# Retention followed by a gated feed-forward block: moving the second tile's attention ticks, two small vector operations and a stream of stores

## The chip, the cores and the metric

The kernel runs on one core of a Trainium2 chip. The metric is the device time of one execution in microseconds. The times shown are medians of several executions.

## The reference

Two blocks follow each other. The first is retention: for each of 8 batches and 8 heads, with 576 positions and a head width of 64, the scores of queries and keys are scaled, multiplied by a decay that falls with the distance and is zero for later positions, and multiplied with the values. The second is a gated feed-forward block on the 4608 x 512 result.

```python
scores = scale * np.matmul(q, k.transpose(0, 1, 3, 2))
ret = scores * Dmat[None, :, :, :]        # gamma_h ** (i - j) for i >= j, else 0
attn_out = np.matmul(ret, v)
x = attn_out.transpose(0, 2, 1, 3).reshape(B * S, H * D)      # 4608 x 512
g, val = x @ w_gate, x @ w_val            # 512 -> 1536 each
out = (g * sigmoid(g) * val) @ w_out      # 1536 -> 512
```

All of it is in float32.

## The kernel before

Every engine works through its instructions in the order in which the Python code writes them (`manual_schedule`), so the place at which a function is called sets what stands behind what on each engine.

**Tiles.** Tokens are worked on in five tiles. The first (n = 0) is computed plainly. The other four (n = 1 to 4, 1024 tokens each) use a fast scheme of matrix multiplication that needs fewer products: each of the three thirds of the hidden columns (`qd` 0 to 2; called thirds 0, 1 and 2 in the text) takes 26 products with the up weights, and the down weights take 26 more. The tables UP and DOWN list, one line a product ("step"), which sums of inputs and weights it needs and what becomes of its result. `up_step` and `down_step` do one step each. One of the four PSUM banks takes the product; VectorE, ScalarE and GpSimd add it into partial results.

**The second tile is special.** At n = 1 the sums of the up weights are formed for the first time, by GpSimd (`w_sums`, L785 and L953) and ScalarE (`negated`, L943, which writes the negated operand into the very slot in which GpSimd then makes the sum). They lie in 13 slots, and slots 8 and higher are used again several times in a third. As each step's operand is used, it is also stored to DRAM (`up_ops`, L986), from where the later tiles fetch it. So a slot may be overwritten only when its store has landed. In the UP table the operand of step 13, for instance, is slot 9; line 15 has `nad 9 1 3`, which overwrites slot 9 for step 18; line 16 makes slot 11 for step 19.

The down operands are fetched from DRAM in all tiles (L880, by SyncE, called SP in the profile) into a ring of eight places. In the second tile the first eight fetches are called at the up steps 21, 22 and 25 of third 2.

**Ticks.** Attention for later tiles goes on between the steps. One tick (`tick`) is for one pair of heads of one batch, t: TensorE does the values of pair t-2, the new states of t-1 and the scores of t-1 (L531 to L572); then a list of `pieces` for VectorE and ScalarE is run one by one behind the following steps: `copies`, `outputs` (`to_x`), `own` (mask the scores), `pairs`, `odd`, `evens` with `keys`, then the transposes of the new pair's q and k on VectorE (L489, into qT and kT), and, together with the transpose of k, `next_load(t)`, which calls `load(t + 2)` on SP: eight transfers of q and k (L293), one of k by rows and one of v (L298). The q and k transfers overwrite the buffer that the transposes of pair t have just read. The next tick's scores need qT and kT.

In an up phase a step runs one piece (`part_on`), except next to lines with five or more results (after steps 17 and 18 none); a down step runs three (`go_on(3)`).

**Where the ticks stand.** `merge` spreads ticks evenly among steps. In the second tile third 0 has no ticks; `load` is called there after steps 6 and 14 only. Ticks 12 to 17 fall among the 52 up steps of thirds 1 and 2: before index 0, 9, 17, 26, 35 and 43 of these. Ticks 18 to 21 fall before down steps 2, 7, 13 and 19:

```python
merge((0.0, ticks(done, cut)), (0.5, ups))
if n == 1:
    for i, f in reversed(list(zip((2, 7, 13, 19), ticks(cut, upto), strict=True))):
        downs.insert(i, f)
```

`down_step` begins with the sums of its own line (`hops`, on VectorE, every third step on GpSimd), then the matmuls, then the reads of the bank, then the pieces. `up_step` issues the store right behind the step's matmuls, from ScalarE's queue.

Of the kernel before, what the change touches and what calls it, by code (L numbers as in the profile page):

```python
# [17 lines left out]
ALU = mybir.AluOpType  # L18
# [136 lines left out]
def kernel(  # L155
# [32 lines left out]
    nc = tc.nc  # L188
# [40 lines left out]
    xr, sr = outer[:, 0, 256 : 256 + L], outer[:, 0, 256 + L : 256 + 2 * L]  # L229
# [110 lines left out]
    last_near = const.tile([P, HP, L], F32, name="last_near")  # L340
# [105 lines left out]
    ret_last = const.tile([P, L], F32, name="ret_last")  # L446
# [128 lines left out]
    def masked(i):  # L575
        p, sr, (ret, ret_last, state) = i % HP, last_scores(i), places(i)

        def own():
            nc.vector.tensor_tensor(out=ret, in0=sc, in1=near[:, 2 * p : 2 * p + 2].unsqueeze(2).to_broadcast([P, 2, NFULL, L]),
                                    op=ALU.mult)  # L580

        def copies():
            (nc.vector.tensor_copy if vector(i + 1) else nc.scalar.copy)(out=even, in_=z[:, 0])

        odd_states = state[:, 1:].rearrange("p (c r) d -> p c r d", r=2)[:, :, 1]

        def pairs():

            nc.vector.tensor_tensor(out=ret_last, in0=sr, in1=last_near[:, p], op=ALU.mult)
            at = odd_states  # L590
            nc.vector.scalar_tensor_tensor(out=at, in0=even, scalar=step[:, p : p + 1], in1=z[:, 1], op0=ALU.mult, op1=ALU.add)

        def odd():
            at = odd_states
            for c in range(1, NFULL):
                nc.vector.scalar_tensor_tensor(out=at[:, c], in0=at[:, c - 1], scalar=step[:, HP + p : HP + p + 1],
                                               in1=at[:, c], op0=ALU.mult, op1=ALU.add)

        def evens():
            at = state[:, 0 : NC - 1].rearrange("p (c r) d -> p c r d", r=2)  # L600
            nc.vector.scalar_tensor_tensor(out=at[:, :, 1], in0=at[:, :, 0], scalar=step[:, p : p + 1], in1=even,
                                           op0=ALU.mult, op1=ALU.add)

        return [copies, own, [pairs, odd, evens]]

    def to_x(i):
        b, p = divmod(i, HP)
# [65 lines left out]
    def tick(t, lo=HP, hi=NP, spread=False, then=None):  # L673
        go_on(len(pieces))
        if hi == HP:

            if lo <= t - 1 < hi:
                scores(t - 1, True)
                new_states(t - 1)
                pieces.extend(masked(t - 1))  # L680
                go_on(3)
            if lo <= t - 2 < hi:
                own_values(t - 2)
            for f in transposes(t) if lo <= t < hi else ():
                f()
            if t + 1 == HP:
                split(0)
            if lo <= t - 2 < hi:
                earlier_values(t - 2)
                if t == HP:  # L690
                    rounding(2)
                    rounding(3)
                to_x(t - 2)[0]()
            if t + 1 == HP:
                rounding(0)
            return
        if lo <= t - 2 < hi:
            own_values(t - 2)
        if lo <= t - 1 < hi:
            new_states(t - 1)  # L700
        if lo <= t - 2 < hi:
            earlier_values(t - 2)
        if lo <= t - 1 < hi:
            scores(t - 1, t - 2 < lo)
        if lo <= t - 1 < hi and whole(t - 2) and not whole(t - 1):
            decay(slice(0, H), slice(0, H), half[1])
        copies, *masks = masked(t - 1) if lo <= t - 1 < hi else (lambda: None,)
        keys, *new = transposes(t) if lo <= t < hi else (lambda: None,)
        outputs = to_x(t - 2)[0] if lo <= t - 2 < hi else lambda: None
        late = needed(1) - 4 <= t < needed(1) - 2 or light(t - 2)  # L710
        if late and masks:
            own, (pairs, odd, evens) = masks
            pieces.extend([lambda: (copies(), outputs(), own()), [pairs, odd, lambda: (evens(), keys())]])
        elif late:
            pieces.append(lambda: (copies(), outputs(), keys()))
        else:
            pieces.extend([lambda: (copies(), keys()), outputs])
            pieces.extend(masks)
        if then and new:
            pieces.extend(new[:-1])  # L720
            pieces.append(lambda: (new[-1](), then()))
        else:
            pieces.extend(new)
            pieces.extend([then] if then else [])
        if not spread:
            go_on(len(pieces))
# [239 lines left out]
    def up_step(n, qd, i):  # L966
        label, opens, xslot, _, wslot, _, ops = up[i]
        busy = n == 1
        if qd == 0:
            done = lambda i: X_FIRST + (min(3 * i, 2 * i + 2, i + 6) if busy else i)  # L970
            x_sums(n, done(i), done(i + 1), busy)
        if busy:
            if i > 1:
                w_sums(qd, i)
            w = up_view(qd)(wslot)
        else:
            w = operand()[:, 0:512].rearrange("p (g x) -> p g x", g=2)
        rhs = x_view(n)(xslot)
        b = bank(label, i == 0)
        for gv in range(2):  # L980
            for c in range(2):
                m = nc.tensor.matmul(b[:, gv * TB : (gv + 1) * TB], w[:, gv, ts(c, P)], rhs[:, c, :],  # L982
                                     start=(opens and gv == 0 and c == 0), stop=(c == 1), skip_group_check=True)
        stepped.append(m)
        if busy:
            nc.scalar.dma_start(out=up_ops[qd][i].rearrange("p (g x) -> p g x", g=2), in_=w)  # L986
            if i in (20, 23) and qd + 1 < NQ:
                first_sums(qd + 1, *((0, 2) if i == 20 else (2, 4)))
            if i == 24 and qd + 1 < NQ:
                negated(qd + 1, 1)  # L990
                w_sums(qd + 1, 1)
            if 0 < i < N - 1:
                negated(qd, i + 1)
            if qd + 1 == NQ:
                for _ in range({21: 3, 22: 2, N - 1: 3}.get(i, 0)):
                    fetch()
        else:
            fetch()

        def result(o, src, negative, vector):  # L1000
            s = io[:, (silus[0] % 4) * TB : (silus[0] % 4 + 1) * TB]
            silus[0] += 1
            nc.scalar.activation(out=s, in_=src[:, 0:TB], func=AF.Silu, scale=-1.0 if negative else 1.0)  # L1003
            dst = hid[:, qd, o // 4, o % 4]
            if negative:
                return lambda: nc.vector.scalar_tensor_tensor(out=dst, in0=src[:, TB : 2 * TB], scalar=-1.0, in1=s,  # L1006
                                                              op0=ALU.mult, op1=ALU.mult)
            if vector:
                return lambda: nc.vector.tensor_tensor(out=dst, in0=src[:, TB : 2 * TB], in1=s, op=ALU.mult)
            nc.gpsimd.tensor_tensor(out=dst, in0=src[:, TB : 2 * TB], in1=s, op=ALU.mult)  # L1010

        reads(ops, b, busy, result, i > N // 2)
        if qd + 1 == NQ and i + 1 == N:
            while products:
                products.pop(0)[1]()
        if max(len(line[-1]) for line in up[i : i + 2]) < 5:
            part_on()

    def down_step(n, i):
        label, opens, slot, hops, ops = down[i]  # L1020
        for op in hops:
            add(nc.gpsimd if i % 3 == 1 and op[0] != "nad" else nc.vector, op, hid_view)
        w = operand().rearrange("p (q x) -> p q x", q=NQ)
        lhs = hid_view(slot)
        b = bank(label, i == 0)
# [14 lines left out]
        if n + 1 == NTILE and i + 1 == N:  # L1040
# [6 lines left out]
                queue.dma_start(out=out[rows + m * P : rows + (m + 1) * P, d * TB : (d + 1) * TB], in_=at[:, ts(m, TB)])  # L1047
            return
        reads(ops, b, False, result)
        at = 2 * (i - (N - 1 - X_FIRST // 2))  # L1050
        if 0 <= at < X_FIRST and n + 1 < NTILE:
            x_sums(n + 1, at, at + 2, True)
# [3 lines left out]
    def merge(*lists):  # L1056
        merged = [((i + d) / len(l), j, f) for j, (d, l) in enumerate(lists) for i, f in enumerate(l)]
        for _, _, f in sorted(merged, key=lambda e: e[:2]):
            f()
# [79 lines left out]
    for n in range(1, NTILE):  # L1139
# [10 lines left out]
                                      mybir.DependencyInfo(mybir.DependencyClass.Sync, mybir.DependencyReason.DATA), reason="loads in turn")  # L1150
                    load(FIRST + i // 14)
        downs = [lambda i=i: down_step(n, i) for i in range(N)]
        merge((0.0, ticks(done, cut)), (0.5, ups))
        if n == 1:

            for i, f in reversed(list(zip((2, 7, 13, 19), ticks(cut, upto), strict=True))):
                downs.insert(i, f)
            merge((0.5, downs))
        else:
            merge((0.0, ticks(cut, upto)), (0.5, downs))  # L1160
        done = upto

# [29 lines left out]
```

## Time and profile before

| | |
|---|---|
| median of the runs | 1050.15 us (1048.26 to 1051.46, 3 runs) |
| profiled execution | 1046.57 us, its span 1044.8 us |
| granted TensorE clock | 0.998 |
| second tile, third 0 of up | 175.6 to 222 us |
| second tile, third 1 | 222 to 274.4 us |
| second tile, third 2 | 274.4 to 324.3 us |
| second tile, down | 324.3 to about 406 us |
| stores of the up operands | 78, 256 KB each, 3.0 us from issue to landing |
| fetches of the down operands | 104, 384 KB each, 3.4 us to landing |

Times of the profile are in microseconds from the start of its span. In the timelines, a row has its start, its length, the engine (PE is TensorE's matmuls, PEld its weight loads, DVE VectorE, ACT ScalarE, POOL GpSimd, SP SyncE; a q behind the name means its sequencer, which issues transfers), the line of the code, what is written from what is read, how often, and in brackets the idle time before it with what ended it. In the lists of waits, an engine, the line and what it waited for are followed by the total, the number of times and the longest. A matmul of one step shows as 8 or 12 records. The idle time of an engine that is not the bound costs nothing.

### The profile page before, as it was taken

To read this page: it belongs to the slowest core of one execution; us is meant where nothing else is said; L and a number is where in the kernel's file an instruction comes from. 1 tells how busy PE (TensorE), PEld (TensorE's weight loads), DVE (VectorE), ACT (ScalarE), POOL (GpSimd) and SP (SyncE) were. 2 spreads that over 40 slices of the span, in tenths; PEclk is the share of its full clock that TensorE was granted. 3 is DMA by queue.
4 is the path that set the end of the run, shared out by engine and by line. 5 is a ranking of instruction groups with operands and counts; after the bars stand their busy time and mean duration, and the time that the engine had idled before them with its cause. 6 is when DMAs were issued, how large, how long until landed. Compare 5 with 4: busy or idle time off the path is not lost.

```text
span 1044.8 us, 21507 instructions
## 1 busy us (share of the span) xinstructions
PE 1025.3 (98%) x8448; PEld 842.7 (81%) x8448; DVE 648.1 (62%) x1063; ACT 295.2 (28%) x646; POOL 401.8 (38%) x347
## 2 busy tenths in 40 slices
PE   6999999999999999999999999999999999999998
PEld 5444555888887888888888888888888888888887
DVE  5578878677767857655468786425476644344644
ACT  4365423243633322132322102222120022231110
POOL 2002367767566035712223048312250483222505
PEclk9999999999999999999999999999999999999999
DMA  9999868776779788765676776545554565555553
GB/s 249 243 280 265 195 196 278 196 209 181 199 195 249 204 216 245 196 166 156 184 219 150 221 184 222 153 137 155 152 173 144 150 201 151 152 153 160 181 161 100
DMA packets 310380, 199.10 MB, mean 191 GB/s; under 512 B 220168, under 2 KB 254984, under 8 KB 310280
## 3 DMA queue, kind: packets, MB, share of 16 engines
q1 hardware_dynamic: 279000, 161.51, 57.2%
q10 hardware_dynamic: 31280, 36.22, 10.4%
q8 instruction: 67, 1.10, 0.4%
q14 instruction: 33, 0.27, 0.1%
HBM read 157.56 MB, written 40.11 MB: 189 GB/s over the span
## 4 chain that ended last, share of the span: by engine, by line
PE 79%; DVE 2%; issue 1%; ACT 0%; DMA 0%; ACTq 0%; DVEq 0%
PE bankC L982 13%; PE bankE L982 12%; PE bankA L982 12%; PE bankB L982 12%; PE bankA L1028 6%; PE bankB L1028 6%; PE bankC L1028 6%; PE bankE L1028 6%; PE outer L531 1%; PE inner L572 1%; PE outer L558 1%; PE inner L542 1%; DVE rest L919 1%; DVE rest L785 0%; PE outer L566 0%
## 5 line engine op out<-in xcount | busy, mean ns | idle before, releaser
L919 POOL TENSOR_TENSOR rest<-rest 128x512 f32<-128x512 f32 x65 | 91.7, 1416 | 298.4 <-DVE rest L919 276.8
L1003 ACT ACTIVATE io<-rest 128x256 f32<-128x256 f32 x180 | 74.9, 417 | 321.9 <-DVE rest L919 277.2
L982 PE MATMUL bankC<-rest,arena 128*128 128x256 f32 x544 | 129.0, 380 | 0.0
L982 PE MATMUL bankA<-rest,arena 128*128 128x256 f32 x544 | 128.7, 379 | 0.0
L785 POOL TENSOR_TENSOR arena<-arena 128x512 f32<-128x512 f32 (+1 forms) x72 | 111.8, 1565 | 39.9 <-DMA up<-arena 26.5
L982 PE MATMUL bankE<-rest,arena 128*128 128x256 f32 x512 | 121.4, 380 | 1.0 <-DVE rest L919 1.0
L982 PE MATMUL bankB<-rest,arena 128*128 128x256 f32 x512 | 121.2, 379 | 0.0
L1010 POOL TENSOR_TENSOR arena<-rest,io 128x256 f32<-128x256 f32 x72 | 52.1, 729 | 166.7 <-ACT io L1003 166.7
L982 PEld LDWEIGHTS bankA<-rest,arena 128*128 128x128 f32 x544 | 103.2, 190 | 14.5 <-issue 0.5
L982 PEld LDWEIGHTS bankC<-rest,arena 128*128 128x128 f32 x544 | 102.9, 190 | 14.5 <-POOL arena L785 0.3
L982 PEld LDWEIGHTS bankE<-rest,arena 128*128 128x128 f32 x512 | 97.0, 190 | 14.6 <-DVE rest L919 1.4
L982 PEld LDWEIGHTS bankB<-rest,arena 128*128 128x128 f32 x512 | 97.0, 190 | 13.3
L785 POOL TENSOR_TENSOR rest<-rest 128x256 f32<-128x256 f32 (+1 forms) x66 | 67.8, 1048 | 102.0 <-DVE rest L419 62.0
L919 DVE TENSOR_TENSOR rest<-bankB,rest 128x512 f32<-128x512 f32 x72 | 48.9, 687 | 67.4 <-PE bankB L982 49.3
L919 DVE TENSOR_TENSOR rest<-bankC,rest 128x512 f32<-128x512 f32 x72 | 48.8, 685 | 66.5 <-PE bankC L982 45.6
L919 DVE TENSOR_TENSOR rest<-bankA,rest 128x512 f32<-128x512 f32 x72 | 48.8, 686 | 62.9 <-PE bankA L982 45.5
L919 DVE TENSOR_TENSOR rest<-bankE,rest 128x512 f32<-128x512 f32 x71 | 48.1, 686 | 61.8 <-PE bankE L982 46.6
L1006 DVE SCALAR_TENSOR_TENSOR arena<-rest,io 128x256 f32<-128x256 f32 x84 | 57.2, 682 | 11.3 <-ACT io L1003 11.3
L1028 PE MATMUL bankA<-arena 128*128 128x256 f32 x252 | 58.0, 380 | 1.3 <-DVE arena L785 1.3
L1028 PE MATMUL bankB<-arena 128*128 128x256 f32 x252 | 58.5, 381 | 0.0
L1028 PE MATMUL bankC<-arena 128*128 128x256 f32 x252 | 58.1, 380 | 0.0
L1028 PE MATMUL bankE<-arena 128*128 128x256 f32 x252 | 57.9, 379 | 0.0
(189 smaller groups left out, 1624.6 us busy)
## 6 DMA issues: line engine op xcount, KB each, us to landing
arena<-up SPq DMA_DIRECT2D x234, 256.0 KB, 2.7
arena<-dn SPq DMA_DIRECT2D x104, 384.0 KB, 3.4
up<-arena ACTq DMA_DIRECT2D x78, 256.0 KB, 3.0
dn<-rest SPq DMA_DIRECT2D x78, 128.0 KB, 1.8
out_dram<-rest SPq DMA_DIRECT2D x31, 256.0 KB, 5.6
qk<-in_q_dram SPq DMA_DIRECT2D x108, 72.0 KB, 2.8
qk<-in_k_dram SPq DMA_DIRECT2D x108, 72.0 KB, 2.3
rest<-in_moe_w_out_dram ACTq DMA_DIRECT2D x6, 1024.0 KB, 6.4
```

The source lines that it names most:

```text
L531: m = nc.tensor.matmul(value(i, hl, c), s["v"][rows, at], ret[rows, c % 2 if whole(i) else hl, c // 2], start=start, stop=start, skip_grou ...
L542: nc.tensor.matmul(z[half[hl], r, c], s["kn"][chunk(i, hl, 2 * c + r, i < HP)], s["v"][rows, at], start=True, stop=True, skip_group_check= ...
L558: nc.tensor.matmul(xr[half[hl]] if c + 1 == NC else value(i, hl, c), state[half[hl], c, :], s["qT"][half[hl], column(i, hl, c)], start=Fal ...
L572: nc.tensor.matmul(sc[chunk(i, hl, 2 * c + r)[0], r if whole(i) else hl, c], kT[half[hl], at], qT[half[hl], at], start=True, stop=True, sk ...
L785: eng.tensor_tensor(out=dst, in0=srcs[0], in1=srcs[1], op=ALU.add if op[0] == "add" else ALU.subtract)
L919: eng.tensor_tensor(out=at(op[1]), in0=at(op[2]), in1=at(op[3]), op=ALU.add if op[0] == "add" else ALU.subtract)
L982: m = nc.tensor.matmul(b[:, gv * TB : (gv + 1) * TB], w[:, gv, ts(c, P)], rhs[:, c, :], start=(opens and gv == 0 and c == 0), stop=(c == 1 ...
L1003: nc.scalar.activation(out=s, in_=src[:, 0:TB], func=AF.Silu, scale=-1.0 if negative else 1.0)
L1006: return lambda: nc.vector.scalar_tensor_tensor(out=dst, in0=src[:, TB : 2 * TB], scalar=-1.0, in1=s, op0=ALU.mult, op1=ALU.mult)
L1010: nc.gpsimd.tensor_tensor(out=dst, in0=src[:, TB : 2 * TB], in1=s, op=ALU.mult)
L1028: nc.tensor.matmul(b[:, m * TB : (m + 1) * TB], lhs[:, qd, ts(m, P)], w[:, qd], start=(opens and qd == 0 and m == 0), stop=(qd == NQ - 1), ...
```

## The change

Four things are done.

- The last scores' mask (`ret_last`) becomes a piece of its own, `last`. In the ticks of the second tile it runs with `own`, which now also stands ahead of `outputs`; in later ticks it stays with `pairs`.
- The stores of the up operands are issued by SP instead of ScalarE.
- The sums of down step i + 1 are written behind the reads of step i, ahead of its pieces, in all four tiles (`hid_sums`).
- The second tile's ticks 12 to 17 stand before index 0, 7, 15, 25, 33 and 39 of the 52 up steps, tick 18 before down step 1 instead of 2.

```diff
@@ -584,9 +584,11 @@
 
         odd_states = state[:, 1:].rearrange("p (c r) d -> p c r d", r=2)[:, :, 1]
 
+        def last():
+            nc.vector.tensor_tensor(out=ret_last, in0=sr, in1=last_near[:, p], op=ALU.mult)
+
         def pairs():
 
-            nc.vector.tensor_tensor(out=ret_last, in0=sr, in1=last_near[:, p], op=ALU.mult)
             at = odd_states
             nc.vector.scalar_tensor_tensor(out=at, in0=even, scalar=step[:, p : p + 1], in1=z[:, 1], op0=ALU.mult, op1=ALU.add)
 
@@ -601,7 +603,7 @@
             nc.vector.scalar_tensor_tensor(out=at[:, :, 1], in0=at[:, :, 0], scalar=step[:, p : p + 1], in1=even,
                                            op0=ALU.mult, op1=ALU.add)
 
-        return [copies, own, [pairs, odd, evens]]
+        return [copies, own, [last, pairs, odd, evens]]
 
     def to_x(i):
         b, p = divmod(i, HP)
@@ -709,13 +711,14 @@
         outputs = to_x(t - 2)[0] if lo <= t - 2 < hi else lambda: None
         late = needed(1) - 4 <= t < needed(1) - 2 or light(t - 2)
         if late and masks:
-            own, (pairs, odd, evens) = masks
-            pieces.extend([lambda: (copies(), outputs(), own()), [pairs, odd, lambda: (evens(), keys())]])
+            own, (last, pairs, odd, evens) = masks
+            pieces.extend([lambda: (copies(), own(), last(), outputs()), [pairs, odd, lambda: (evens(), keys())]])
         elif late:
             pieces.append(lambda: (copies(), outputs(), keys()))
         else:
             pieces.extend([lambda: (copies(), keys()), outputs])
-            pieces.extend(masks)
+            for own, (last, pairs, *rest_of) in [masks] if masks else []:
+                pieces.extend([own, [lambda: (last(), pairs()), *rest_of]])
         if then and new:
             pieces.extend(new[:-1])
             pieces.append(lambda: (new[-1](), then()))
@@ -983,7 +986,7 @@
                                      start=(opens and gv == 0 and c == 0), stop=(c == 1), skip_group_check=True)
         stepped.append(m)
         if busy:
-            nc.scalar.dma_start(out=up_ops[qd][i].rearrange("p (g x) -> p g x", g=2), in_=w)
+            nc.sync.dma_start(out=up_ops[qd][i].rearrange("p (g x) -> p g x", g=2), in_=w)
             if i in (20, 23) and qd + 1 < NQ:
                 first_sums(qd + 1, *((0, 2) if i == 20 else (2, 4)))
             if i == 24 and qd + 1 < NQ:
@@ -1016,10 +1019,14 @@
         if max(len(line[-1]) for line in up[i : i + 2]) < 5:
             part_on()
 
+    def hid_sums(i):
+        for op in down[i][3]:
+            add(nc.gpsimd if i % 3 == 1 and op[0] != "nad" else nc.vector, op, hid_view)
+
     def down_step(n, i):
         label, opens, slot, hops, ops = down[i]
-        for op in hops:
-            add(nc.gpsimd if i % 3 == 1 and op[0] != "nad" else nc.vector, op, hid_view)
+        if i == 0:
+            hid_sums(0)
         w = operand().rearrange("p (q x) -> p q x", q=NQ)
         lhs = hid_view(slot)
         b = bank(label, i == 0)
@@ -1047,6 +1054,8 @@
                 queue.dma_start(out=out[rows + m * P : rows + (m + 1) * P, d * TB : (d + 1) * TB], in_=at[:, ts(m, TB)])
             return
         reads(ops, b, False, result)
+        if i + 1 < N:
+            hid_sums(i + 1)
         at = 2 * (i - (N - 1 - X_FIRST // 2))
         if 0 <= at < X_FIRST and n + 1 < NTILE:
             x_sums(n + 1, at, at + 2, True)
@@ -1150,13 +1159,16 @@
                                       mybir.DependencyInfo(mybir.DependencyClass.Sync, mybir.DependencyReason.DATA), reason="loads in turn")
                     load(FIRST + i // 14)
         downs = [lambda i=i: down_step(n, i) for i in range(N)]
-        merge((0.0, ticks(done, cut)), (0.5, ups))
         if n == 1:
 
-            for i, f in reversed(list(zip((2, 7, 13, 19), ticks(cut, upto), strict=True))):
+            for i, f in reversed(list(zip((0, 7, 15, 25, 33, 39), ticks(done, cut), strict=True))):
+                ups.insert(i, f)
+            merge((0.5, ups))
+            for i, f in reversed(list(zip((1, 7, 13, 19), ticks(cut, upto), strict=True))):
                 downs.insert(i, f)
             merge((0.5, downs))
         else:
+            merge((0.0, ticks(done, cut)), (0.5, ups))
             merge((0.0, ticks(cut, upto)), (0.5, downs))
         done = upto
```

In the order of the built program, SP then has a `load` after steps 2, 12 and 22 of third 1 (before: 2, 14, 24) and after steps 4, 12 and 20 of third 2 (before: 5, 14, 24), and the store of the step that follows stands behind each.

## The prediction

> **What bounds the kernel now.** I read the page's busy times and chain first, then the waits of TensorE alone, then the timelines of the second tile (175.6 to about 406 us of the span), where all but one part of the change lies. From the page:
>
> ```profile
> PE 1025.3 (98%) x8448; PEld 842.7 (81%) x8448; DVE 648.1 (62%) x1063; ACT 295.2 (28%) x646; POOL 401.8 (38%) x347
> PE 79%; DVE 2%; issue 1%; ACT 0%; DMA 0%; ACTq 0%; DVEq 0%
> ```
>
> TensorE is the bound. The change leaves its 4240 matmuls as they are, so it can only remove or add holes. The second tile's holes, in the table of TensorE's waits (us in total, times, longest):
>
> ```profile
> PE inner L572 <- issue: 2.3, 1, 2.3
> PE bankA L1028 <- DVE arena L785: 1.3, 1, 1.3
> PE outer L566 <- DVE kT L489: 1.1, 1, 1.1
> PE bankE L982 <- DVE rest L919: 1.0, 1, 1.0
> ```
>
> They lie at 331.9, 360.7, 272.6 and 191.3 us; from 406 us on TensorE is full except at the very end. Together they are 5.8 us: all that can be won, 0.55%.
>
> What can be lost shows in SP. Its waits have the line below, and its timeline one whole `load` (start, us):
>
> ```profile
> SPq L293 <- DVE kT L489: 95.5, 19, 13.6
> ...
> 313.98 8.77 SPq L880 DMA_DIRECT2D arena<-dn  x5
> 327.78 2.21 SPq L293 DMA_DIRECT2D qk<-in_q_dram  x4
> 330.04 2.18 SPq L293 DMA_DIRECT2D qk<-in_k_dram  x4
> 332.26 1.47 SPq L298 DMA_DIRECT2D kn<-in_k_dram  x1
> 333.78 0.62 SPq L298 DMA_DIRECT2D v<-in_v_dram  x1
> ```
>
> A `load` first holds SP until VectorE has transposed kT (the buffer it overwrites), then for 6.6 us of issuing (5.3 to 5.8 where kn takes 0.4 to 0.5 us as in the other ticks; I use 5.8). Now the way of one store, step 13 of third 1, through the timelines of ACT, POOL and PE (step 19 is the last line):
>
> ```profile
> 248.43 0.33 ACTq L986 DMA_DIRECT2D up<-arena  x1
> 250.54 0.63 ACT L943 ACTIVATE arena<-arena 128x512 f32<-128x512 f32 x1
> 251.25 1.27 POOL L953 TENSOR_TENSOR arena<-arena 128x512 f32<-128x512 f32 x1 [3.61 <-ACT arena L943]
> 253.21 2.74 POOL L919 TENSOR_TENSOR rest<-rest 128x512 f32<-128x512 f32 x2 [0.68 <-DVE rest L919]
> 255.90 1.27 POOL L785 TENSOR_TENSOR arena<-arena 128x512 f32<-128x512 f32 x1
> 258.64 1.89 PE L982 MATMUL bankE<-rest,arena 128*128 128x256 f32 x8
> ```
>
> The store reads slot 9 of the weights' sums. Slot 9 is then overwritten for step 18 (ACT negates, POOL subtracts), and POOL makes step 19's operand only after that and two more sums: at 257.2, with TensorE there at 258.6. The spare time is 1.4 us. That these engines do wait for landings, the same waits between 175 and 325 us say:
>
> ```profile
> POOL arena L785 <- DMA up<-arena: 26.5, 9, 5.1
> ACT arena L943 <- DMA up<-arena: 14.4, 7, 4.2
> ```
>
> **What the Trainium skill says.** DMA: Bandwidth & Descriptors, "Anatomy of one DMA": a DMA's semaphore waits are held on the sequencer that issues it, the DMA engines never wait. The trace agrees: the 95.5 us above are SP's own. The same page, "Issuing engines are not separate DMA queues": SP and ACT feed the same 16 engines, and two issuers save only issuing time. The trace has both queues (161.51 and 36.22 MB) but no run here shows them merged. Runtime: NRT & Kernel Launch, "Instruction fetch mechanics": instructions come in 16 KiB blocks of 256, the next fetched while the current runs. The instruction queue's 67 packets of 1.10 MB agree, and I take the hole of 2.31 us inside a tick's matmuls, which nothing released, for a block that came late.
>
> **The change part by part.** Steps of a third start 1.73 us apart (256.91, 258.64, 260.36); a full tick takes 2.56 us, tick 13, which has no values to do, 1.4.
>
> Down sums a step ahead: the same additions stand ahead of the next pieces of a tick instead of behind them. The hole of 1.35 us at 360.7 goes; cover for the pieces that are now later is a down step of 2.6 us: gain 1.4 with crumbs.
>
> Last scores masked earlier: one VectorE row of 0.23 us a tick, behind `own` instead of ahead of `pairs`. TensorE waits for neither: nothing, both ways within 0.2.
>
> Ticks at other steps: pieces run one per step (none after steps 17 and 18 of a third), `load` with the last. Ticks 13 to 17 move 2, 2, 1, 2 and 4 steps ahead. Tick 15 gets two steps instead of one between kT and its scores: the 1.1 us goes. Tick 17 now follows tick 16's kT with none between: a new wait of 0 to 2.5 us (from 1.1 with one step, plus 1.73, less what VectorE is quicker there); it falls into item 4 below and isn't counted twice. The late block of instructions may or may not come again, as the boundaries fall elsewhere: half, 1.2. The bank wait at 191.3 follows ACT, which loses its stores: half, 0.5. Gains in all: 4.2 (2.5 to 5.8).
>
> Stores on SP: ACT loses 78 issues of mostly 0.33 to 0.6 us; ACT is busy 16 to 23 us of each third of about 50, so that alone gives no more than the 0.5. On SP each store stands in program order behind any `load` issued at an earlier step. A `load` follows steps 2, 12 and 22 of third 1 and 4, 12 and 20 of third 2. The time from the step's end to kT was, before, 1.2, 3.4, 4.8, 3.8, 1.9 and 5.3 us (SP's start of L293 less the end of TensorE's step); for the new places I take 1.2, 2.5, 4, 2.5, 2 and 3. A store lands 3.0 us after issue (page, median), dn 3.4. From the end of the step:
>
> 1. Third 1, after step 2: store 3 leaves at 1.2 + 5.8 + 0.3 = 7.3, lands 10.3; negation and sum (0.63 + 1.27 + 0.1) to 12.3. It is step 8's operand, due at 5 steps + tick 13 = 10.0. Cost 2.3.
> 2. After step 12: store 13 leaves at 8.6, lands 11.6, sum of step 18 at 13.6, then 2.74 + 1.27 on POOL: 17.6. Step 19 is due at 6 steps + tick 14 = 12.9. Cost 4.7.
> 3. Third 2, after step 4: store 6 leaves at 9.1, lands 12.1, sum at 14.1; step 10 is due at 5 steps + tick 16 = 11.2. Cost 2.9.
> 4. After step 12: as 2 with kT at 2.0: 17.1 against 12.9. Cost 4.2.
> 5. After step 20: here the first down operands (L880) also stand behind the `load`; before, they went ahead of it, at 313.98. The first leaves at 3 + 5.8 + 0.5 = 9.3, lands 12.7; down step 0 is due 5 steps on, at 8.6. Cost 4.1.
> 6. The two `load`s of third 0 (after steps 6 and 14) and the one after step 22: spare time about equals the delay; 1 in all.
>
> Sum 19.2. Less 4.2: +15.0. The profiled execution took 1046.6 (span 1044.8 and 1.8 around it): 1061.6. The median of the runs lies 3.6 above that execution, so 1065.
>
> Bounds: stores landing in 2.0 us and kT half a us sooner take about 1.6 from each of items 1 to 5 (11 left, less 5.8: +5); landing in 5 us, which the timeline's v transfers of 4.4 us (page) ahead of them in the same queue allow, adds 2 to each (29, less 2.5: +27).
>
> **The rivals.** *The spare time holds (faster).* POOL and ACT are idle for half of the tile, and third 1's other sums have 3 to 4 us in hand. If kT came at once and the queue cleared within 4 us of a step's end, every item but 2 would vanish and the holes alone would decide: 1046. Deciding point: a store no more than 2 us later than ACT issued it. Against it: 5.8 us of issuing alone is over that.
>
> *Only the ticks count.* Stores turn out free, tick 17's wait and item 5's late operand give back the gains: about 1050, the same. Against it is the same figure.
>
> *The wait spreads (much slower).* ACT's negation waits for the landing in program order, and the SiLUs behind it, VectorE's products and the reading of banks wait with it; kT is then later and the next `load` too. Each item grows by 3 us or more: 1080 to 1090. For it: ACT waited 277 us for VectorE over the span, so the two are closely coupled; against it: TensorE's holes let VectorE catch up.
>
> *The change does not do what it says*: the order of the built program shows SP's stores and `load`s as counted here, so none.
>
> **How the numbers follow.** The chief case (+5 to +27, 1055 to 1077) 0.74; much slower 0.10; slower by less than 5 us 0.04; the same 0.04; faster 0.08. What a measurement can tell from no change is about 0.3%, 3.2 us. Range 1053 to 1079, which leaves out the faster and same cases and most of the much slower one.
>
> **What would show it.** TensorE's waits should get new rows at L982 of 2 to 5 us whose releaser is POOL's or ACT's arena rows, and one at the first L1028 for the dn transfer, or for SP; SP's timeline should show the stores bunched behind each `load`, 0.4 us apart. The rows of 1.3 (L785) and 1.1 (kT, tick 15) should be gone. I am wrong if third 1 and third 2 still take about 52 and 50 us, or if the new holes stand where no store or operand was behind a `load`.

## The result and the profile after

The changed kernel takes 1085.3 us (median; 1085.06 to 1090.14, 4 runs) against 1049.2 us for the kernel before on the same chip: a ratio of 1.0357 with a 95% interval of 1.0317 to 1.0396. Forecast were 1065 and a range up to 1079. The direction was right, the size was not: +36 us instead of +15. The profiled execution took 1085.25 us with a span of 1083.5, which is 38.7 us over that of before.

In the changed file lines stand some three to seven further down: the up matmul L982 is L985 there, the down matmul L1028 is L1035, POOL's sums L785 and L953 are L788 and L956, ACT's negation L943 is L946, the bank's readers L919 are L922. From the page of after, the busy times, the granted clock in 40 slices of the span, and the chain that ended last:

```profile
PE 1037.3 (96%) x8448; PEld 848.0 (78%) x8448; DVE 661.3 (61%) x1063; ACT 294.1 (27%) x646; POOL 404.9 (37%) x347
...
PEclk9999999998888899999999999999999999999999
...
PE 82%; DVE 4%; DMA 4%; SPq 4%; POOL 3%; issue 2%; ACT 1%; DVEq 0%; ACTq 0%; POOLq 0%
```

Two things are to be seen. The chain now runs through SP's queue, a landing and POOL's sums, which had no share before. And TensorE, with the same 8448 matmuls, is busy for 12.0 us more than before (1025.3): some matmuls became slower. The five slices with an 8 in the row of the clock, from 244 to 379 us, say where.

The thirds and the down steps of the second tile, each with its length, TensorE's busy time first and the granted clock near the end of the row, third from last (the bounds are round figures; the thirds begin at 176.6, 224.2 and 292.3 us, the first down step comes at 365.4):

```profile
175.60:222.00 46.40, 44.59 (x202) 37.63 (x201) 35.97 (x47) 15.96 (x33) 32.40 (x24) 1.00 0.78 235
222.00:290.00 68.00, 57.54 (x527) 47.92 (x528) 47.00 (x64) 21.57 (x50) 34.99 (x27) 0.90 0.47 134
290.00:361.00 71.00, 57.62 (x524) 48.22 (x518) 45.19 (x68) 24.39 (x59) 32.16 (x25) 0.90 0.57 150
361.00:446.00 85.00, 80.50 (x940) 70.12 (x944) 57.12 (x82) 18.78 (x54) 24.15 (x14) 0.96 0.79 220
```

Third 0 is about as before. Thirds 1 and 2 take 68.2 us and, to the end of the last step, 66.6 us; before they took 52.4 and 49.9. The loss lies in the second tile, and there where `load`s are called. TensorE's waits after:

```profile
PE bankA L1035 <- DMA arena<-dn: 6.5, 1, 6.5
PE bankA L985 <- POOL arena L956: 6.1, 1, 6.1
PE bankC L985 <- POOL arena L956: 4.6, 1, 4.6
...
PE bankB L985 <- DVE rest L922: 3.9, 2, 2.5
PE bankB L985 <- POOL arena L956: 3.2, 1, 3.2
PE bankE L985 <- POOL arena L956: 2.8, 1, 2.8
```

Four rows are up matmuls that POOL's sums release, and the first is down step 0, released by the first down operand. The fourth row shown, a bank that VectorE had not read yet, was not foreseen in that size: its longer wait is 2.55 us. The rows of before for L785 (1.3) and for a matmul record inside a tick (2.3) are gone.

One of these holes followed through the engines, in the timelines of after. SP: the `load` after step 2 of third 1, which ended at 229.34:

```profile
230.39 1.96 SPq L293 DMA_DIRECT2D qk<-in_q_dram  x4
232.39 2.74 SPq L293 DMA_DIRECT2D qk<-in_k_dram  x4
235.23 0.45 SPq L298 DMA_DIRECT2D kn<-in_k_dram  x1
235.78 0.61 SPq L298 DMA_DIRECT2D v<-in_v_dram  x1
236.47 4.04 SPq L989 DMA_DIRECT2D up<-arena  x5
```

ACT, whose negation overwrites the slot that the first of these stores reads:

```profile
240.65 0.63 ACT L946 ACTIVATE arena<-arena 128x512 f32<-128x512 f32 x1 [8.80 <-DMA up<-arena]
```

POOL, which makes step 8's operand in that slot:

```profile
241.36 1.27 POOL L956 TENSOR_TENSOR arena<-arena 128x512 f32<-128x512 f32 x1 [10.50 <-ACT arena L946]
```

And TensorE, at steps 7, 8 and 9:

```profile
237.53 1.99 PE L985 MATMUL bankC<-rest,arena 128*128 128x256 f32 x8
242.68 3.67 PE L985 MATMUL bankB<-rest,arena 128*128 128x256 f32 x8 [3.15 <-POOL arena L956]
246.19 1.89 PE L985 MATMUL bankA<-rest,arena 128*128 128x256 f32 x8
```

The store of step 3 stands behind 6 us of issuing, its slot is free 4.2 us after the start of its own issue (of which issuing takes 1.1), and step 8 comes 3.15 us late. The last fence shows what the forecast left out: step 8 itself takes 3.67 us instead of 1.89. The wait of 3.15 us costs 1.8 us more behind it.

### The profile page after: what moved, and what is told of

Same layout as the page of the kernel before. It is cut to its first block, busy times and chain, and to the rows that moved or that the text cites. A ratio compares the mean times of both kernels' runs of the same rounds, so it can differ in the third digit from the quotient of the medians.

```text
span 1083.5 us, 21526 instructions
## 1 busy us (share of the span) xinstructions
PE 1037.3 (96%) x8448; PEld 848.0 (78%) x8448; DVE 661.3 (61%) x1063; ACT 294.1 (27%) x646; POOL 404.9 (37%) x347
## 4 chain that ended last, share of the span: by engine, by line
PE 82%; DVE 4%; DMA 4%; SPq 4%; POOL 3%; issue 2%; ACT 1%; DVEq 0%; ACTq 0%; POOLq 0%
PE bankA L985 11%; PE bankE L985 11%; PE bankB L985 11%; PE bankC L985 11%; PE bankA L1035 6%; PE bankB L1035 6%; PE bankE L1035 6%; PE bankC L1035 6%; SPq L293 2%; PE bankC L754 2%; PE bankA L754 1%; PE bankE L754 1%; PE bankB L754 1%; PE outer L531 1%; DMA up<-arena 1%
## 5 line engine op out<-in xcount | busy, mean ns | idle before, releaser
L922 POOL TENSOR_TENSOR rest<-rest 128x512 f32<-128x512 f32 x65 | 91.9, 1418 | 303.3 <-DVE rest L922 284.8
L985 PE MATMUL bankA<-rest,arena 128*128 128x256 f32 x544 | 132.7, 388 | 7.7 <-POOL arena L956 6.1
L788 POOL TENSOR_TENSOR arena<-arena 128x512 f32<-128x512 f32 (+1 forms) x72 | 114.4, 1601 | 45.4 <-DMA up<-arena 31.0
L985 PE MATMUL bankC<-rest,arena 128*128 128x256 f32 x544 | 129.2, 380 | 0.0
L985 PE MATMUL bankB<-rest,arena 128*128 128x256 f32 x512 | 123.2, 384 | 4.5 <-POOL arena L956 3.2
L985 PEld LDWEIGHTS bankA<-rest,arena 128*128 128x128 f32 x544 | 106.0, 195 | 24.7 <-POOL arena L956 6.5
L985 PE MATMUL bankE<-rest,arena 128*128 128x256 f32 x512 | 121.8, 381 | 0.2 <-POOL arena L788 0.2
L985 PEld LDWEIGHTS bankC<-rest,arena 128*128 128x128 f32 x544 | 102.7, 190 | 14.7 <-POOL arena L788 0.3
L985 PEld LDWEIGHTS bankB<-rest,arena 128*128 128x128 f32 x512 | 98.3, 193 | 19.0 <-POOL arena L956 3.6
L985 PEld LDWEIGHTS bankE<-rest,arena 128*128 128x128 f32 x512 | 97.0, 190 | 14.7 <-POOL arena L788 1.1
L788 POOL TENSOR_TENSOR rest<-rest 128x256 f32<-128x256 f32 (+1 forms) x66 | 68.1, 1053 | 103.2 <-DVE rest L419 64.2
L922 DVE TENSOR_TENSOR rest<-bankC,rest 128x512 f32<-128x512 f32 x72 | 48.9, 687 | 67.8 <-PE bankC L985 47.7
L922 DVE TENSOR_TENSOR rest<-bankB,rest 128x512 f32<-128x512 f32 x72 | 48.8, 685 | 63.6 <-PE bankB L985 47.4
L922 DVE TENSOR_TENSOR rest<-bankA,rest 128x512 f32<-128x512 f32 x72 | 48.8, 686 | 60.1 <-PE bankA L985 42.8
L922 DVE TENSOR_TENSOR rest<-bankE,rest 128x512 f32<-128x512 f32 x71 | 48.1, 685 | 60.1 <-PE bankE L985 45.4
L1009 DVE SCALAR_TENSOR_TENSOR arena<-rest,io 128x256 f32<-128x256 f32 x84 | 61.1, 729 | 10.8 <-ACT io L1006 10.8
L1035 PE MATMUL bankA<-arena 128*128 128x256 f32 x252 | 59.8, 388 | 6.5 <-DMA arena<-dn 6.5
L1035 PEld LDWEIGHTS bankA<-arena 128*128 128x128 f32 x252 | 49.0, 195 | 13.9 <-DVE rest L788 6.9
L1035 PE MATMUL bankB<-arena 128*128 128x256 f32 x252 | 58.5, 381 | 0.1
L1035 PE MATMUL bankC<-arena 128*128 128x256 f32 x252 | 58.0, 380 | 0.0
```

The costliest lines, as they stand in the source:

```text
L788: eng.tensor_tensor(out=dst, in0=srcs[0], in1=srcs[1], op=ALU.add if op[0] == "add" else ALU.subtract)
L922: eng.tensor_tensor(out=at(op[1]), in0=at(op[2]), in1=at(op[3]), op=ALU.add if op[0] == "add" else ALU.subtract)
L1035: nc.tensor.matmul(b[:, m * TB : (m + 1) * TB], lhs[:, qd, ts(m, P)], w[:, qd], start=(opens and qd == 0 and m == 0), stop=(qd == NQ - 1), ...
```

## The experiments

Ratios are to the kernel before on the same chip. Where slow matmuls are counted, a matmul is slow if the next starts 0.43 us after it and not 0.216 us; each loses 0.211 us. A missing record looks the same, so a count may be one too high.

**The stores alone.** Before, with one line of the change:

```diff
-            nc.scalar.dma_start(out=up_ops[qd][i].rearrange("p (g x) -> p g x", g=2), in_=w)
+            nc.sync.dma_start(out=up_ops[qd][i].rearrange("p (g x) -> p g x", g=2), in_=w)
```

> The kernel before with one edit: SP issues the up operands' stores. Ticks stand where they stood, so a load follows steps 2, 14, 24 of third 1 and 5, 14, 24 of third 2, and the first five down fetches still go ahead of the last load. Theory (stores held behind loads on SP, ended by holes on TensorE, and each hole over about 2.5 us followed by 3.4 us or more at half clock): holes of 3 to 6 us after step 2 and after step 5, smaller ones or none after the steps 14 (the slots stored next are not soon overwritten), none at down step 0: 12 to 20 us slower than before, about 1062 to 1069. Rival 1 (the tick places do the harm): within 3 us of before. Rival 2 (SP is slow at stores wherever a load stands): as slow as the full change, 1085.

Measured: 1062.8 us, ratio 1.0131 (1.0102 to 1.0161). TensorE's waits of this kernel:

```profile
PE bankA L982 <- POOL arena L953: 6.6, 1, 6.6
...
PE bankB L982 <- POOL arena L953: 3.4, 1, 3.4
PE outer L566 <- DVE kT L489: 2.4, 2, 1.9
PE inner L572 <- issue: 2.0, 1, 2.0
PE bankA L1028 <- DVE arena L785: 1.3, 1, 1.3
PE bankC L982 <- POOL arena L785: 1.3, 1, 1.3
```

Two of the holes are there: that of step 8 in third 1 (`load` after step 2) and that of third 2 behind the `load` after step 5. None lies behind the `load`s after step 14 of either third, and none at down step 0. 18 slow matmuls follow the two and seven more the hole of 2.0 us inside a tick, together 5.3 us. Two smaller waits are larger or new: tick 15's for kT grew from 1.1 to 1.9 us, and step 6 of third 2 waits 1.3 us for a sum.

**All but the stores, and the ticks alone.** The first is the changed kernel with the stores on ACT; the second is the kernel before with only this:

```diff
-        merge((0.0, ticks(done, cut)), (0.5, ups))
         if n == 1:
-            for i, f in reversed(list(zip((2, 7, 13, 19), ticks(cut, upto), strict=True))):
+            for i, f in reversed(list(zip((0, 7, 15, 25, 33, 39), ticks(done, cut), strict=True))):
+                ups.insert(i, f)
+            merge((0.5, ups))
+            for i, f in reversed(list(zip((1, 7, 13, 19), ticks(cut, upto), strict=True))):
                 downs.insert(i, f)
             merge((0.5, downs))
         else:
+            merge((0.0, ticks(done, cut)), (0.5, ups))
...
```

> The changed kernel with the stores back on ACT. Theory: one hole of 3 to 7 us at the first down step, whose operand is fetched behind the load of tick 17, and its clock loss of about 2 us; the old holes at kT, down sums and instruction block are gone (4.8 us): 1048 to 1054. Rival 1 (tick places do the harm): 1070 or more. Rival 2 (stores cost nothing by themselves, the whole is an interaction): about 1049 as well, and then the stores alone must be near before too.

> The kernel before with the tick places alone. Theory: as the run without stores, 1.4 us later for the hole of the down sums that stays: 1049 to 1056, with a hole at the first down step and none at tick 15's kT. Rival (tick places do the harm): 1070 or more.

Measured: 1058.6 us, ratio 1.0099 (1.0068 to 1.0130), and 1059.1 us, 1.0102 (1.0078 to 1.0127). In the waits of the first:

```profile
PE bankA L1035 <- DMA arena<-dn: 7.7, 1, 7.7
...
PE bankB L985 <- DVE rest L922: 2.6, 1, 2.6
...
PE bankA L985 <- POOL arena L788: 1.9, 2, 1.6
```

The second has the same 7.7 and 2.6. Seven matmuls are slow in the first, 13 in the second. So the new tick places alone bring two larger holes without a single store on SP: down step 0, whose operands SP fetches behind the `load` after step 20, and the bank wait at step 23 of third 1. A third wait, of 1.5 to 1.6 us for a sum of L788 (L785 in the second) at step 22 of third 2, comes with them. No up matmul waits for a sum of L956. Both kernels are slower than was expected of them; the bank wait was in neither expectation.

**The sums and masks alone.** Before, with `hid_sums` a step ahead and `last` as its own piece (both as in the change's diff).

> The kernel before with the down sums a step ahead and the last scores' mask moved, ticks and stores as before. Theory: the 1.35 us wait at the down sums goes, nothing else changes: 1 to 2 us faster, which may not be told from no change. Rival: the pieces behind the sums come late for a tick and cost 1 to 3 us.

Measured: 1048.5 us, ratio 1.0005 (0.9988 to 1.0022): nothing that can be told. The down sums' hole of 1.35 us is gone in its trace, while a bank wait in third 0 grew from 1.0 to 2.4 us and one of 0.9 us stands at another down step.

The three parts alone add +1.3%, +1.0% and 0; together they give +3.6%. The missing 1.2%, some 12.5 us, needs, by where the holes stand, both: `load`s after step 12 instead of 14 **and** stores behind them. There after has its hole of 4.55 us in third 1 and its waits of 5.2 us in all in third 2, each with slow matmuls, and there none of the single parts has one.

**The loads taken apart.** The changed kernel, stores on SP and all ticks in their new places; but the ten transfers of each `load` of ticks 12 to 17 are put in a list, and from the third step after the call on every step issues two of them behind its own store:

```diff
+        class Late:
+            def dma_start(self, **kw):
+                later.append(lambda: nc.sync.dma_start(**kw))
...
             nc.sync.dma_start(out=up_ops[qd][i].rearrange("p (g x) -> p g x", g=2), in_=w)
...
+            some_loads()
...
-            load(t + AHEAD)
+            if FIRST <= t < FIRST + 6:
+                late_loads.extend([None] * HOLD)
+                load(t + AHEAD, late_loads)
+            else:
+                load(t + AHEAD)
+
+    def some_loads():
+        if late_loads and late_loads[0] is None:
+            late_loads.pop(0)
+            return
+        for _ in range(min(2, len(late_loads))):
+            late_loads.pop(0)()
```

> The changed kernel, but each load of ticks 12 to 17 is issued in pieces of two transfers, one piece behind the store of each following step, from the third step on; same transfers, same SP queue, same results. Theory (a store is late because a whole load stands ahead of it on SP, waiting for kT and issuing): the holes behind POOL's sums and at the first down step go, what is left is the bank wait of about 2.6 us and a kT wait that the tick places bring: 1047 to 1053. Rival 1 (stores land late because they share SP's queue with the many small packets of the loads, whatever the order): holes behind POOL's sums stay at 3 us or more, 1060 or slower. Rival 2 (ACT without stores or the tick places do the harm): 1060 or slower, with holes at other releasers.

Measured: 1048.5 us, ratio 0.9988 (0.9978 to 0.9999). With the order of this one queue changed, all 36 us are gone. SP's timeline, at the place shown above for after (L275 are the pieces of the `load`, L995 the stores):

```profile
229.20 0.87 SPq L275 DMA_DIRECT2D qk<-in_q_dram  x2
230.16 0.45 SPq L995 DMA_DIRECT2D up<-arena  x1
230.66 1.08 SPq L275 DMA_DIRECT2D qk<-in_q_dram  x2
231.85 0.67 SPq L995 DMA_DIRECT2D up<-arena  x1
232.56 1.85 SPq L275 DMA_DIRECT2D qk<-in_k_dram  x2
234.51 0.44 SPq L995 DMA_DIRECT2D up<-arena  x1
```

Each store now has at most two transfers between it and the store before. SP still waits for kT at the first pair of a `load`, but the stores of three more steps go out ahead of that wait, and it is shorter. SP's waits for kT in thirds 1 and 2, of after (222 to 360 us) and of this kernel (222 to 330 us):

```profile
SPq L293 <- DVE kT L489: 42.7, 6, 8.4
...
SPq L275 <- DVE kT L495: 20.4, 5, 5.1
```

TensorE's longest waits in the second tile:

```profile
PE bankB L991 <- DVE rest L928: 2.5, 1, 2.5
PE bankA L991 <- POOL arena L794: 1.9, 2, 1.6
```

The bank wait stays, and so does the wait of 1.6 us at step 22 of third 2. The ticks alone have both, so they are the ticks' own and no matter of the stores. No sum of the L956 kind and no down operand is waited for any more.

**The down operands first.** The changed kernel, with two fetches ahead of the `load` after step 20:

```diff
-                for _ in range({21: 3, 22: 2, N - 1: 3}.get(i, 0)):
+                for _ in range({20: 2, 21: 1, 22: 2, N - 1: 3}.get(i, 0)):
```

> The changed kernel with two of the first down fetches called one step earlier, at step 20 of third 2, so that they go ahead of tick 17's load. Theory: the hole of 6.5 us at the first down step and the half clock behind it (about 1.7 to 2) go, all else stays: 1076 to 1079. Rival (the fetch waits for its ring place, not for SP): 1085 as the changed kernel.

Measured: 1075.5 us, ratio 1.0232 (1.0202 to 1.0262), 10 us less than after (7.4 us between the two profiled executions). The wait of 6.5 us at down step 0 is gone; the next step has one of 1.6 us for a sum of VectorE. The larger holes in thirds 1 and 2 stay, at 2.5 to 5.6 us. So this hole is SP's order too, and independent of the others.

**What a hole costs behind it.** The kernel before with 14 stops of TensorE in the last two tiles, which have no holes of their own. At a stop, GpSimd does a few short multiplications on a spare tile after the last step's matmul, and TensorE waits for them:

```diff
+        for n in range(times):
+            m = nc.gpsimd.tensor_scalar(out=idle, in0=idle, scalar1=1.0, scalar2=None, op0=ALU.mult)
+            if n == 0:
+                link(m, stepped[-1])
+        link(nc.tensor.nop(), m)
```

> The kernel before with fourteen stops of TensorE put into the up steps of tiles 3 and 4 (it waits for 2 to 12 small operations that GpSimd does for nothing), of about 1.5 to 8 us, 17 us apart. Theory (a hole itself halves the clock behind it): no slow matmuls behind holes up to about 2.3 us, matmuls of 0.43 instead of 0.22 us for 3.4 us or more behind those of 3.4 us or more, either behind those between; each such hole costs 1.7 us or more above its own length. Rival (the half clock belongs to the loads or stores of the second tile): no matmul of 0.43 us behind any of these holes.

Measured, one execution: 1156.9 us, the granted clock 0.957. Two places in TensorE's timeline of this kernel, a hole of 3.25 us and one of 2.16 us:

```profile
694.82 3.75 PE L997 MATMUL bankB<-x_odd,arena 128*128 128x256 f32 x8 [3.25 <-issue]
698.36 3.00 PE L997 MATMUL bankC<-rest,arena 128*128 128x256 f32 x8
701.20 1.89 PE L997 MATMUL bankA<-rest,arena 128*128 128x256 f32 x8
...
940.20 1.97 PE L997 MATMUL bankE<-rest,arena 128*128 128x256 f32 x8 [2.16 <-issue]
942.00 1.89 PE L997 MATMUL bankB<-rest,arena 128*128 128x256 f32 x8
```

Behind the first, a step and a half run at about half speed; behind the second, none. All 14:

| hole, us | 2.16 | 2.63 | 2.77 | 3.17 | 3.25 | 3.79 | 5.23 | 6.05 | 6.39 | 6.63 | 7.24 | 7.79 | 10.2 | 10.8 |
|---|---|---|---|---|---|---|---|---|---|---|---|---|---|---|
| slow matmuls | 0 | 7 | 0 | 8 | 13 | 8 | 8 | 11 | 7 | 10 | 12 | 13 | 12 | 12 |

From 3.2 us on every hole brought 7 to 13 slow matmuls, 1.5 to 2.7 us more; the number hardly grows with the hole. Of the two at 2.6 and 2.8 us one brought seven and one none. Together 121 slow matmuls, 25.5 us.

**Pieces of loads with the old ticks.** Stores, sums and masks of the change and the loads taken apart, but the ticks at their places of before.

> As the run with loads in pieces, with the ticks at their places of before: stores on SP, down sums a step ahead, masks moved, loads in pieces. Theory: no hole behind POOL's sums, no bank wait; the kT wait of tick 15 and perhaps the late instruction block come back: 1044 to 1049, the same as before or up to 0.5% faster. Rival 1 (stores land late in SP's queue): 1055 or slower.

Measured: 1051.2 us, ratio 1.0014 (0.9997 to 1.0031), between the range of the theory and that of the rival. No up matmul waits for a sum, as in the theory. The bank wait of 2.55 us is gone with the new places, and the old kT wait (1.6) and the hole inside a tick's matmuls (2.9) are back:

```profile
PE inner L578 <- issue: 2.9, 1, 2.9
...
PE outer L572 <- DVE kT L495: 1.6, 1, 1.6
```

**A version for both.** The loads taken apart, with ticks at the old places except for one step more between tick 15's kT and its scores, and with tick 18 before down step 1:

```diff
-            for i, f in reversed(list(zip((0, 7, 15, 25, 33, 39), ticks(done, cut), strict=True))):
+            for i, f in reversed(list(zip((0, 9, 17, 27, 35, 43), ticks(done, cut), strict=True))):
```

> The changed kernel with the loads of ticks 12 to 17 issued two transfers a step behind the stores, and with its tick places replaced: before index 0, 9, 17, 27, 35 and 43 of the up steps (those of the kernel before, but tick 15 one step later), tick 18 before down step 1. If each remaining hole belongs to a place - the bank wait of 2.55 us to tick 15 at index 25, the kT wait of 1.6 us to the single step between tick 15's kT and its scores at index 26, the 2 to 2.9 us inside tick 18's scores to its standing at down step 2 - all three are gone, about 1 us of small waits is left, no half clock, and the span is 1042 to 1044: a ratio of 0.995 to 0.997 to the kernel before. If the bank wait follows from the later sums and masks or from SP's stores rather than from the place, it shows again in third 1 at 2 to 2.6 us and the ratio is 0.998 to 1.000. If the late block of instructions does not depend on tick 18's place, a hole of 2 us or more without releaser shows at the start of the down steps.

Measured: 1048.6 us, ratio 0.9997 (0.9982 to 1.0012). All three holes are gone as the first theory has it, but the gain it counted is not there. A hole of 3.3 us, with seven slow matmuls behind it, stands among the down steps. ACT's timeline there:

```profile
356.12 0.81 ACT L627 COPY x_odd<-outer 128x128 f32<-128x128 f32 x3
363.01 0.96 ACT L512 ACTIVATE kn<-kn,tab 128x256 f32<-128x256 f32 x2 [6.08 <-DMA kn<-in_k_dram]
...
364.84 0.59 ACT L925 COPY rest<-bankB 128x512 f32<-128x512 f32 x1
```

The last `load`, called late and issued in pieces, left its kn until 357.2. ACT waited for it, and the read of a bank (L925) stood behind in program order. The delay that keeps the stores on time had made this `load` itself late. An earlier call of that one load was not tried. No version tried is faster than the kernel before by as much as 0.3%; the loads taken apart come nearest, with 0.12% (0.01 to 0.22).

## Why the prediction was right in kind and wrong in size

**Right: SP's program order is the cause.** Each of the five larger holes foreseen was there, released by what was named (in items 2 and 4 TensorE stopped at step 18 already and not only at step 19), and taking the `load`s apart removed them all with everything else of the change in place. The Trainium skill (DMA: Bandwidth & Descriptors, "Issuing engines are not separate DMA queues") says that a second issuer saves only issuing time, usually small beside the transfer. That is the gain of a second issuer, and not the price of the order within one. Here the stores behind a `load` land in 3.3 to 4.1 us, but leave only 7 to 12 us after the step ahead of the `load` has ended, and that order cost 36 us.

**Wrong, the step that failed: the sum took a hole for its length.** "The change leaves its 4240 matmuls as they are, so it can only remove or add holes" is false. (The page counts 8448 matmul records before and after; 4240 stands in no view.) The matmuls stayed the same, but not their time. Behind the new holes TensorE ran at half clock: 47 slow matmuls in the second tile, 9.9 us, none of which the forecast has and no rival either. The Trainium skill states this (TensorE: Matmul & The Clock Gate, "Part 1: The HAM clock gate"): after an idle window of about 3.4 us the clock is halved until a busy one has passed. The trace agrees with the length: the six stretches at half clock in the second tile are 3.4 or 6.8 us long, parts of them inside the holes. Two of them and what follows each (bounds, length, TensorE's busy time, then the granted clock):

```profile
242.70:246.11 3.41, 3.41 (x8) 0.50 0.45 157
246.11:266.59 20.48, 18.24 (x209) 1.00 0.49 121
266.59:273.42 6.83, 4.31 (x9) 0.50 0.44 161
273.42:280.00 6.58, 6.58 (x32) 1.00 0.45 159
```

As an estimate from that page's window, 3.4 us at half clock cost 1.7 us, so items 2, 4 and 5, which the forecast put at 4.1 to 4.7 us, should each have carried 1.7 us more, some 5 in all. With the measured 9.9 us added, +15 would have been +25 and 1075, inside the range; without them the measurement would have been, at 1075. The holes' own excess below, 7.3 us, is the second part of the miss; without it alone the measurement would have been 1078, just inside.

**Right in place, too small: items 1 to 5.** In us from the end of the step (the landing from the start of its issue); the forecast's values, or what follows from them, in brackets:

| item (`load` after) | kT ready after | `load` issued in | the store or fetch leaves at | and lands in | hole |
|---|---|---|---|---|---|
| 1, third 1, step 2 | 1.0 (1.2) | 6.0 (5.8) | 7.1 (7.3) | 4.1 (3.0) | 3.15 (2.3) |
| 2, third 1, step 12 | 3.7 (2.5) | 6.1 (5.8) | 9.9 (8.6) | 3.9 (3.0) | 4.55 (4.7) |
| 3, third 2, step 4 | 3.8 (2.5) | 6.7 (5.8) | 11.9 (9.1) | 3.3 (3.0) | 6.07 (2.9) |
| 4, third 2, step 12 | 3.2 (2.0) | 6.4 (5.8) | 9.6 (8.1) | 4.0 (3.0) | 5.2 (4.2) |
| 5, third 2, step 20 | 3.8 (3) | 5.5 (5.8) | 10.6 (9.3) | 4.5 (3.4) | 6.52 (4.1) |

Item 4 is three waits: 1.25 for tick 17's kT, 2.78 and 1.17 behind the store. The five are 25.5 us against 18.2. Three terms are off. kT came about 1 us later at four of the new places than guessed from the places of before. The first transfer behind a `load` took 1.1 to 1.2 us to issue, where most of those behind it took 0.3 to 0.7. In items 1, 2 and 4 it is the store that counts, and its longer issue is most of the 0.9 to 1.1 us by which the landing, counted from the start of the issue, exceeds the 3.0 of the forecast; in items 3 and 5 it stands ahead of the transfer that counts. And item 5's fetch landed 1.1 us later than its median of before. The median of the stores, which I took, is of stores issued from another queue than the `load`s; the landings of items 1, 2 and 4 lie halfway to the forecast's upper bound of 5 us. In item 2 step 18 came 4.55 us late already; the 4 us that POOL then needs for step 19 lay behind step 18's own 3.8 us at half clock, so the hole came out near the forecast by another way.

**Not foreseen: the bank wait of 2.55 us** at step 23 of third 1. The forecast asked what the new tick places do to kT, and not what they do to VectorE's reading of the banks. The wait comes with the tick places alone, and is gone with the old places and with tick 15 before index 27 instead of 25. Why VectorE is late there was not followed.

**The gains.** The down sums' 1.35 and tick 15's 1.1 us went as counted. The hole of 2.3 us inside a tick's matmuls was gone altogether, where half was counted. Five kernels with tick 18 before down step 2 have it (2.0 to 2.9 us) and six with it before down step 1 have not: it belongs to a place in the instruction stream, as supposed, though that a block of instructions is what came late was not shown. The half us at 191.3 did not come: the waits for a bank there went from 1.0 to 1.8.

**The ledger** of the profiled executions: holes at items 1 to 5, 25.5; the bank wait and one small wait, 2.75; third 0, +0.8; slow matmuls, 9.9; less 4.75 of old holes: 34.2 of the 38.7 us. Of the rest about 1 us was there at the start of the second tile; the other 3.5 are not assigned. About 2 of these are busy time, which grew by 12.0 us where the slow matmuls account for 9.9.

**The rivals.** "The wait spreads" has the right time (1080 to 1090), and not for its reason: the negations did hold ACT, and the later kT fits that, but item 1, the first in the tile, grew by 0.85 us and no item but one by 3 us. "The spare time holds" and "only the ticks count" fell; the ticks alone cost 1% instead of being even.

## What to carry to other kernels

Before a stream is moved to another issuing queue, list what stands ahead of each of its members there, waits included, and compare with the time until its buffer is wanted; if a long item is in the way, cut it into pieces and put the stream between them, but then ask whether the pieces have become late themselves. Price a hole on TensorE with the slow matmuls behind it. Two parts that cost about 1% each can cost more than their sum, here 3.6%, when one uses up the spare time on which the other depends.

## What was not expected of the hardware

The half clock began with holes shorter than the 3.4 us of the Trainium skill's window (TensorE: Matmul & The Clock Gate, "Part 1: The HAM clock gate"); here the measurement decides. Between steps, single holes of up to 2.4 us had no slow matmul behind them. The bank wait of 2.55 us had seven or eight in four kernels and none in a fifth, holes of 2.60 and 2.63 us had seven each, one of 2.77 us none, and from 3.1 us on every one had some. Inside a tick, among its short matmuls, even two holes of 2.0 us had seven, and others of 2.0 and 2.3 us none. The price, 1.5 to 2.7 us in the run of 14 stops, depends little on the length, so two holes of 3.2 us cost more than one of 6.4.
